# Gate and up products in swapping 64-row tiles, with a new order of work, in a transformer block of linear-memory attention and a gated feed-forward

## The chip, the cores and the metric

The kernel runs on one NeuronCore of a Trainium2 chip. The metric is the device time of one execution in microseconds. The engines are named as the profile names them: PE is TensorE (matmul), PEld its weight loads, DVE is VectorE, ACT is ScalarE, POOL is GpSimd, SP is SyncE, which here issues DMAs.

## What is computed

The input x is 2048 rows of 448 values in bfloat16. It is normalised, goes through an attention with a memory carried over four segments of 512 rows, and through a gated feed-forward of width 1792; the two results are multiplied and added to x.

```python
xn = layernorm(x)
# attention, 16 heads of 28, segments s = 0..3 of 512 rows
q, k, v = xn @ wq, xn @ wk, xn @ wv
phi = lambda t: where(t > 0, t + 1, exp(t))
for s in range(4):
    p = softmax(qs @ ks.T * 28**-0.5 + causal_mask)
    a_mem = (phi(qs) @ M) / (phi(qs) @ z + 1e-6)
    o = g * a_mem + (1 - g) * (p @ vs)
    M, z = M + phi(ks).T @ vs, z + phi(ks).sum()
s = o @ wo
g = silu((gelu(xn @ w_gate) * (xn @ w_up)) @ w_down)
return x + s * g
```

## The kernel before

Everything is done by segments of 512 rows. A segment has 4 blocks of 128 rows. The 448 input columns are the contraction of the projections and of gate/up: three chunks of 128 rows of weights and a rest of 64.

The work is written as about a thousand small operations (class `Op`, line 26), each with its engine or engines, an estimated time, the operations that it needs, the buffers that it takes and a priority. The function `arrange` (line 276) is a list scheduler that runs when the program is built: it plays the operations against estimated engine times, takes at each step the one of best priority among those that could start within `AHEAD`, assigns buffers and PSUM banks, and returns the operations in order of their planned start. They are issued to the engines' queues in that order, so each queue's order is fixed, and a wait that comes out longer on the chip than planned holds all that is behind it on that engine. Two tables steer this: `PRIO` (line 87) gives a priority to each operation by name, and `STEP` (line 258) says after which step of the attention's scores a piece of PE work may start. They were found by a search over the planner's own time.

The stages follow each other as G0, A0, A1, G1, A2, G2, A3, G3, D3 (`ORDER`, line 273).

- An A stage (`attention`, from line 960) is ten steps of scores (line 985, four heads at once in 32-row tiles), each followed by exps on ACT (line 1000), masks on POOL (line 1011), and four groups of products with v (line 1047, four 32-column tiles). The probabilities go to `pt` buffers, five of them. Between the scores PE does other work: projections of a later segment (line 714), the down products of an earlier one (line 1155), the output projection (line 1185), the memory's update (line 860) and read (line 898).
- A G stage (`gate_up`, from line 1070) makes 14 blocks of 128 hidden columns. Each block takes two PSUM banks, one for gate and one for up. `full` (line 1089) does 3 chunks for gate and 3 for up, each with all 128 rows. `halves` (line 1104) does the rest of 64 rows: gate's rest lies on partitions 0 to 63 and up's on 64 to 127 of `wh_sb`, so that the two matmuls use different row tiles of the array. Four blocks' halves are done together, so that the array's tiling changes rarely: two blocks end with them and two begin with them (`VISITS`). Then ACT does the gelu (line 1114) and DVE multiplies it by up (line 1119) into `hT`.
- The projections of a segment come in pairs of blocks: 3 full chunks for each of the two (`Unit.full`), and one visit in which the two rests of 64 rows run side by side (`visit`, lines 714 to 754). Each is evicted by DVE or ACT.
- D3 is the last segment's down product and output, block by block; the last block is cut in three.

At the start, `layer_norm` of segment 0 makes two forms of x: x less its mean (`xc`, line 663), which is known early, and the normalised x (`xn`, line 653), which waits for the variance and a power on POOL (line 646). Each of the four blocks is turned by four PE transposes (line 596) and copied to `xcT` or `xnT` (line 598). All projections of segment 0 use `xcT`, and the missing factor is put in when they are evicted (lines 752 and 754); gate/up uses `xnT`. Later segments are turned by DMA transposes on SP's queue (line 685).

The first loads are issued at line 490: the first two blocks of x and the other weights by SP, the last two blocks of x and `wv` in three pieces by ACT. Each of the four segments has its own x buffer; the loads for segments 2 and 3 (line 561) are issued after the last transpose of segment 1. The residual add reads that buffer again (line 1176) at the end of each segment's work.

The planner takes 1.65 or 2.25 us from a DMA's issue to its landing, and 1.3 us of SP's queue for a DMA transpose.

```python
def halves(ends, begins):
    def mm():
        for fc in ends + begins:
            for i in range(2):
                r = slice(i * HALF, (i + 1) * HALF)
                nc.tensor.matmul(out=bf[fc].ap(i), lhsT=wh_sb[r, fc * P:(fc + 1) * P],
                                 rhs=xT.ap()[r, NC3, :], start=fc in begins, stop=fc in ends)
```

Of the kernel before, what the change touches and what calls it, by code (L numbers as in the profile page):

```python
# [15 lines left out]
ORDER = mybir.DependencyInfo(mybir.DependencyClass.NoSync, mybir.DependencyReason.DATA)  # L16
# [9 lines left out]
class Op:  # L26


    def __init__(self, name, eng, fn, deps=(), after=(), prio=0.0, mode=None, act=None, acq=(),
                 uses=(), alone=False, kb=None, rate=240.0):  # L30
        self.alone, self.kb, self.rate = alone, kb, rate
        self.name, self.eng, self.fn, self.prio = name, eng, fn, prio
        self.mode, self.act, self.acq = mode, act, list(acq)
        self.deps = [d for d in deps if d is not None]
        self.after = [d for d in after if d is not None]
        self.start = self.done = self.on = None
        for b in list(uses) + self.acq:
            b.users.append(self)
# [15 lines left out]
class Buf:  # L54
# [221 lines left out]
def arrange(ops):  # L276
# [11 lines left out]
    while ready:  # L288
# [24 lines left out]
        if e == "PE" and o.mode and o.mode != mode:  # L313
            s, mode = s + SWITCH, o.mode
# [1423 lines left out]
```

## Time and profile before

| | |
|---|---|
| time, three runs | 229.37, 230.7, 234.46 us; median 230.7 |
| span of the profiled execution, first to last instruction | 227.6 us |
| the profiled execution's own time | not shown apart; the median is 3.1 us above the span |
| PE busy | 217.5 us, 96% of the span |
| ACT, DVE, POOL busy | 152.7, 152.7, 129.3 us |
| PE clock granted | 1.0 in nearly the whole span |

A profile row in order of time gives start, length, engine, line, operation and how many were merged. A matmul's length includes its way through the array, so lengths of neighbours overlap: what a matmul costs is the distance to the next start. Brackets give the idle time of the engine before the row and what ended it. In a row of groups the numbers after the bar are the busy time in us, the mean in ns, and the idle time before. A few matmul records can be missing, so a merged row may count one matmul too few.

### The profile page before, as it was taken

The page shows a single profiled execution, that of the slowest core. Times are in us where ns is not written, and L with a number is a line of the kernel's source. Part 1 is how long each engine was busy: PE and PEld are TensorE (multiplying, and loading weights), DVE is VectorE, ACT ScalarE, POOL GpSimd, SP SyncE. Part 2 cuts the span into 40 slices and gives each one's busy share as a digit, 9 for nine tenths or more (in the row PEclk, how much of TensorE's full clock was granted, in tenths as well). Part 3 has the DMA queues.
Part 4 walks back from the last instruction along what each step waited for, and adds up shares of the span by engine and source line. Part 5 has one row for each costly group of instructions (what it writes and reads, how often), then busy time and mean ns, then how long its engine had stood idle before and what let it go on. Part 6 is the DMA issues. An engine that isn't in the chain of part 4 may idle for free.

```text
span 227.6 us, 4462 instructions
## 1 busy us (share of the span) xinstructions
PE 217.5 (96%) x1557; PEld 95.6 (42%) x1570; DVE 152.7 (67%) x287; ACT 152.7 (67%) x212; POOL 129.3 (57%) x221
## 2 busy tenths in 40 slices
PE   7999999889999999999999999999999999999991
PEld 2544433333544434344444444344444434444561
DVE  3799998767965795674875587863746463647262
ACT  4799645999898779432788898443878875346120
POOL 8601400579588599603599989853199477604500
PEclk9999999999999999999999999999999999999999
DMA  6999569964434763217603132272500018135011
GB/s 215 222 357 259 103 152 248 237 128 83 48 72 72 183 127 74 76 38 201 186 20 68 27 71 69 59 196 59 140 1 4 12 45 225 31 84 125 4 40 50
DMA packets 44708, 25.11 MB, mean 110 GB/s; under 512 B 30808, under 2 KB 40856, under 8 KB 44680
## 3 DMA queue, kind: packets, MB, share of 16 engines
q1 hardware_dynamic: 43704, 24.05, 44.7%
q10 hardware_dynamic: 976, 0.71, 1.0%
q8 instruction: 14, 0.23, 0.4%
q14 instruction: 14, 0.11, 0.2%
HBM read 16.00 MB, written 2.98 MB: 83 GB/s over the span
## 4 chain that ended last, share of the span: by engine, by line
PE 82%; ACT 10%; DVE 2%; issue 2%; ACTq 1%; POOL 1%; DVEq 0%; POOLq 0%
PE ps L1155 16%; PE ps L1089 15%; PE pp L1089 14%; PE ps L714 11%; PE pp L985 5%; PE ps L1185 5%; PE ps L1047 4%; ACT pt L1000 3%; PE ps L1104 3%; PE pp L1104 3%; PE pp L1155 2%; ACT pt L1248 2%; PE ps L898 1%; PE ps L860 1%; PE ps L1221 1%
## 5 line engine op out<-in xcount | busy, mean ns | idle before, releaser
L1000 ACT ACTIVATE pt<-pp 128x1024 bf16<-128x1024 f32 x75 | 73.3, 1037 | 11.8 <-PE pp L985 9.9
L1011 POOL TENSOR_SCALAR_AFFINE_SELECT pt<-pt 128x256 bf16<-128x256 bf16 x128 | 54.3, 448 | 26.0 <-ACT pt L1000 23.6
L1155 PE MATMUL ps<-wd_sb,hT 128*128 128x448 bf16 x182 | 39.0, 354 | 0.4 <-DVE qs L750 0.4
L1114 ACT ACTIVATE gl<-pp 128x512 bf16<-128x512 f32 x28 | 15.8, 595 | 29.0 <-PE pp L1104 23.2
L1155 PEld LDWEIGHTS <-hT 128*128 128x128 bf16 x210 | 18.8, 98 | 20.1 <-issue 5.0
L1119 DVE TENSOR_TENSOR hT<-gl,pp 128x512 bf16<-128x512 bf16 x28 | 18.4, 682 | 11.6 <-ACT gl L1114 11.5
L1119 DVE TENSOR_TENSOR hT<-gl,ps 128x512 bf16<-128x512 bf16 x28 | 18.7, 677 | 11.0 <-ACT gl L1114 8.4
L1114 ACT ACTIVATE gl<-ps 128x512 bf16<-128x512 f32 x28 | 16.6, 597 | 13.0 <-PE ps L1089 6.1
L1089 PEld LDWEIGHTS <-wu_sb 128*128 128x128 bf16 x168 | 16.4, 98 | 20.1 <-issue 0.3
L1089 PEld LDWEIGHTS <-wg_sb 128*128 128x128 bf16 x168 | 14.9, 98 | 22.5 <-issue 7.1
L909 POOL TENSOR_TENSOR om<-om,rb 128x512 f32<-128x512 f32 x12 | 14.9, 1268 | 15.9 <-DMA rb<-rdr 15.8
L714 PEld LDWEIGHTS <-xnT 128*128 128x128 bf16 (+1 forms) x192 | 15.0, 96 | 20.6 <-issue 10.1
L1089 PE MATMUL pp<-xnT,wu_sb 128*128 128x512 bf16 x84 | 22.7, 379 | 0.3
L1089 PE MATMUL ps<-xnT,wu_sb 128*128 128x512 bf16 x83 | 22.5, 379 | 0.2
L956 POOL TENSOR_TENSOR oT<-oa,om 128x512 bf16<-128x512 f32 x12 | 16.0, 1337 | 11.5 <-DVE oa L953 11.5
L1089 PE MATMUL ps<-xnT,wg_sb 128*128 128x512 bf16 x81 | 22.1, 380 | 0.3 <-issue 0.3
L1089 PE MATMUL pp<-xnT,wg_sb 128*128 128x512 bf16 x76 | 21.2, 380 | 0.4 <-issue 0.3
L831 POOL TENSOR_SCALAR e<-e 128x896 bf16<-128x896 bf16 (+1 forms) x12 | 12.8, 1070 | 10.9 <-ACT e L826 10.9
L985 PE MATMUL pp<-qT,kT 32*128 32x512 bf16 (+3 forms) x238 | 17.0, 301 | 2.0 <-ACT pt L1000 1.8
L646 POOL TENSOR_TENSOR rs<-rs,nhalf 128x1 f32<-128x1 f32 (+1 forms) x7 | 6.1, 882 | 16.1 <-DVE rs L641 16.1
L883 DVE COPY oa<-ps 128x512 f32<-128x512 f32 x16 | 10.9, 683 | 5.2 <-PE ps L1047 5.0
L1176 POOL TENSOR_TENSOR oo<-sg,x_sb 128x448 bf16<-128x448 f32 x12 | 12.4, 1037 | 2.7 <-DVE sg L1196 2.7
(121 smaller groups left out, 325.3 us busy)
## 6 DMA issues: line engine op xcount, KB each, us to landing
rb<-rdr SPq DMA_DIRECT2D x28, 256.0 KB
out_dram<-oo SPq DMA_DIRECT2D x15, 112.0 KB
wd_sb<-in_B_w_down_dram SPq DMA_DIRECT2D x2, 784.0 KB
x_sb<-in_A_x_dram SPq DMA_DIRECT2D x3, 448.0 KB
rdr<-dc SPq DMA_DIRECT2D x28, 32.0 KB
wg_sb<-in_B_w_gate_dram SPq DMA_DIRECT2D x2, 384.0 KB
wu_sb<-in_B_w_up_dram SPq DMA_DIRECT2D x2, 384.0 KB
wg_sb<-in_B_w_gate_dram SPq DMA_DIRECT2D x1, 576.0 KB
```

Source lines behind the costliest of these rows:

```text
L714: nc.tensor.matmul(out=self.bank.ap()[:, 0:D], lhsT=self.xT.ap()[r, c, n * P:(n + 1) * P], rhs=self.w[r, c, :], **kw)
L831: o = gps(f"mi{nm}{s}{half}", n / 1024, lambda: nc.gpsimd.tensor_scalar(out=t(), in0=t(), scalar1=1.0, scalar2=0.0, op0=ALU.min, op1=ALU.max),
L909: oU[s, g, 1] = t, gps(f"sm{s}{g}", 1.22, lambda t=t, r=r: nc.gpsimd.tensor_tensor(out=t.ap(), in0=t.ap(), in1=r.ap(), op=ALU.mult), deps= ...
L956: oT[s][1].append(gps(f"cb{s}{g}", 1.22, lambda g=g, t=t, tm=tm: nc.gpsimd.tensor_tensor(out=dst.ap()[:, g, :], in0=t.ap(), in1=tm.ap(), o ...
L985: nc.tensor.matmul(out=S2[i // 2].ap(i % 2)[:, c0:c0 + n], lhsT=kT[s][0].ap()[r, g, kb * P:(kb + 1) * P], rhs=qT[s][0].ap()[r, g, kb * P:L ...
L1000: nc.scalar.activation(out=dst, in_=src, func=ACT.Exp, scale=scale)
L1011: nc.gpsimd.affine_select(out=v, in_=v, pattern=[[0, 2], [1, P]], compare_op=ALU.is_ge, fill=0.0, base=0, channel_multiplier=-1)
L1089: nc.tensor.matmul(out=bf[fc].ap(i), lhsT=w[:, c, fc * P:(fc + 1) * P], rhs=xT.ap()[:, c, :], start=begins and c == 0, stop=not begins and ...
L1104: nc.tensor.matmul(out=bf[fc].ap(i), lhsT=wh_sb[r, fc * P:(fc + 1) * P], rhs=xT.ap()[r, NC3, :], start=fc in begins, stop=fc in ends)
L1114: a = act(f"ge{s}{fc}", L, lambda: nc.scalar.activation(out=gl.ap(), in_=bf[fc].ap(0), func=ACT.Gelu_apprx_tanh), func="gelu", deps=[o], a ...
L1119: nc.vector.tensor_tensor(out=hT[s][0].ap()[:, fc, :], in0=gl.ap(), in1=bf[fc].ap(1), op=ALU.mult), deps=[a] + held,
L1155: nc.tensor.matmul(out=bank.ap()[:, 0:D], lhsT=hT[s][0].ap()[:, fc, b * P:(b + 1) * P], rhs=wd_sb[:, fc, :], start=(fc == 0), stop=(fc == ...
```

## The change

1. **Gate/up.** `full` and `halves` go. Each block of hidden columns has two parts, both in 64-row tiles. Turn 0 does four chunks (three and the rest): gate on rows 0 to 63 and up on rows 64 to 127 of each chunk. Turn 1 does three chunks with the roles swapped: up on rows 0 to 63, gate on 64 to 127. The parts are interleaved: turn 0 of the next block stands before turn 1 of this one. Since turn 1 adds to the same PSUM banks from the other row tile, a one-element ACT operation (`turn_over`, planned at 0.2 us) waits for the end of turn 0 on both tiles, and turn 1 waits for it. A table `BANKS` says which pairs of banks a block may take.
2. **Projections.** A pair of blocks is one PE operation of six full chunks and one 64-row pair; the 64-row pair comes first if the array is not in the full tiling at that place, last otherwise (`flex`, `tail_first`).
3. **Segment 0.** Only blocks 0 and 2 have a centred form (`EARLY`); blocks 1 and 3 are projected from the normalised x. After each of the two groups of centred transposes stands an idle 512-column matmul (`wm`). PSUM for this part may be any of eight banks. The small pieces of `wv` are loaded by SP, not by ACT.
4. **Buffers.** Three x buffers in place of four: segment 3's x takes segment 0's. Six `pt` buffers in place of five.
5. **Order.** DMA estimates become 1.9 or 2.5 us to landing, 1.38 us for a DMA transpose (1.9 for two kinds of segment 0), engines begin at 0.8 us. The exps of phi are all held by score steps. `PRIO` and `STEP` are searched anew and all entries differ; a small term breaks ties.

The diff, cut to its core (the tables left out):

```diff
-SEM, SWITCH, TABLE, AHEAD, LATE = 0.06, 0.1, 1.29, 0.2, 0.3
+SEM, SWITCH, TABLE, AHEAD, LATE, BEGIN = 0.06, 0.1, 1.29, 0.2, 0.3, 0.8
+EARLY = (0, 2)
...
-        if e == "PE" and o.mode and o.mode != mode:
+        if e == "PE" and o.flex:
+            o.tail_first = mode != "full"
+            s, mode = s + SWITCH * (mode not in ("full", "r64")), "full" if o.tail_first else "r64"
+        elif e == "PE" and o.mode and o.mode != mode:
...
-        xs = tiles(NSEG, [P, NB, D], BF16, "x_sb")
+        x_p = slots(NSEG - 1, [P, NB, D], BF16, "x_sb")
+        xb = [Buf(x_p, [(s % (NSEG - 1),)]) for s in range(NSEG)]
...
-        pt_p = slots(5, [P, HG, L], BF16, "pt")
+        pt_p = slots(6, [P, HG, L], BF16, "pt")
...
-            return op(name, {"SP": (0.62, 1.65 if kb < 200 else 2.25)}, fn, kb=kb, **kw)
+            return op(name, {"SP": (0.62, 1.9 if kb < 200 else 2.5)}, fn, kb=kb, **kw)
...
-            return op(name, {"SP": (1.3, 1.5)}, fn, kb=200, **kw)
+            t = 1.9 if name[:3] in ("tk0", "tq0") else 1.38
+            return op(name, {"SP": (t, t + 0.9)}, fn, kb=200, **kw)
...
-                for b in range(NB):
+                for b in EARLY:
                     centred = dve(f"xc{b}", 0.32, lambda b=b: nc.vector.tensor_scalar(
...
+                    kept_warm.append(pe(f"wm{b}", [L], lambda bank=bank: nc.tensor.matmul(
+                        out=bank.ap(), lhsT=warm[:, 0:P], rhs=warm, start=True, stop=True), deps=[warm_in], after=[o],
...
-                self.scaled = s == 0
+                self.scaled = s == 0 and n in EARLY
...
+                    for c in range(NC3 + 1 - turn):
                         for i in range(2):
+                            w = wh_sb if c == NC3 else (wg_sb, wu_sb)[i ^ turn][:, c, :]
+                            m = nc.tensor.matmul(out=bf[fc].ap(i ^ turn), lhsT=w[side[i], fc * P:(fc + 1) * P],
+                                                 rhs=xT.ap()[side[i], c, :], start=not turn and c == 0,
+                                                 stop=turn == 1 and c == NC3 - 1)
+                            if not turn:
+                                ended[fc, i] = m
+                            elif c == 0:
+                                ordered(m, turns[fc])
...
+                    def turn_over():
+                        turns[fc] = nc.scalar.activation(out=idle[0:1, :], in_=nhalf[0:1, 0:1], func=ACT.Identity)
+                        for i in range(2):
+                            ordered(turns[fc], ended[fc, i])
+                    swapped[fc] = op(f"ty{s}{fc}", {"ACT": (0.2, 0.25)}, turn_over, deps=[prev], after=[nhalf_in], prio=at(ph, fc) - 401)
...
-            for ends, begins in VISITS:
-                for fc in ends:
-                    full(fc, True)
-                h = halves(ends, begins)
-                for fc in ends:
-                    hidden(fc, h)
-                for fc in begins:
-                    a = hidden(fc, full(fc, False))
+            part(0, 0)
+            for fc in range(NFC):
+                if fc < NFC - 1:
+                    part(fc + 1, 0)
+                h = part(fc, 1)
+                a = hidden(fc, h)
```

More of the change, by code (lines that the diff above doesn't have):

```diff
@@ L276, in arrange @@
 def arrange(ops):
[L279 removed]
+    free = {e: BEGIN for o in ops for e in o.eng}
     mode, table = "full", "exp"
@@ L404, in fast_path @@
         END = ONE + [(0,), (2,)]
+        EIGHT = [(i,) for i in range(8)]
         APART = [(i, j) for i in range(4, 8) for j in range(i + 1, 8)]
@@ L567, in fast_path @@
         table_op = op("table", {"ACT": (1.5, 1.6)}, lambda: nc.scalar.activation(
-            out=igate[:, 0:1], in_=nhalf[:, 0:1], func=ACT.Exp), deps=[nhalf_in], after=wv_in, prio=-400)
+            out=igate[:, 0:1], in_=nhalf[:, 0:1], func=ACT.Exp), deps=[nhalf_in], after=wv_in[:1], prio=-400)
         def warm_up():
@@ L717, in needs @@
             def needs(self, rest):
-                return self.w_in[slice(1, None) if rest else slice(0, 1)] + [self.xd[self.n]]
+                return self.w_in[slice(1, None) if rest else slice(0, 1)] + [
+                    self.xd[EARLY.index(self.n) if self.scaled else self.n]]
             def full(self):
@@ L807, in project, with mm, tails @@
                 us = [Unit(s, nm, n, -8400.0) for nm, n in pair]
-                fs = [u.full() for u in us]
-                o = visit("wr{}{}{}".format(s, *pair[0]), us, -9500.0)
-                ahead = dict(fulls=[(f, len(f.after)) for f in fs], visit=o, sc=sc, step=k)
-                pairs_ahead.append(ahead)
-        pairs_ahead = []
+                def mm(us=us):
+                    def tails(first):
+                        for u in us:
+                            u.product(NC3, start=first, stop=not first)
+                    first = o_of[us[0]].tail_first
+                    if first:
+                        tails(True)
+                    for u in us:
+                        for c in range(NC3):
+                            u.product(c, start=not first and c == 0, stop=first and c == NC3 - 1)
+                    if not first:
+                        tails(False)
+                u, nm = us[0], pair[0][0]
+                new = not u.dst[2:] and nm != "wq"
+                ns = [D] * (2 * NC3 + 1)
+                occ = sum(n / 2400 + 0.0025 for n in ns) + SWITCH
+                o = op("pj{}{}{}".format(s, *pair[0]), {"PE": (occ, occ + 0.17)}, mm, mode="full", flex=True,
+                       deps=sum((x.needs(False) + x.needs(True) for x in us), []), prio=-8400.0,
+                       acq=[x.bank for x in us] + ([u.dst[0]] if new else []), uses=[u.xT], after=u.dst[2:3])
+                o_of[u] = o
+                if new:
+                    u.dst.append(o)
+                for x in us:
+                    x.out(o)
+                pairs_of.append((o, sc, k))
+        o_of, pairs_of = {}, []
         tabled, phis = [], []
@@ L1071, in fast_path, with ordered @@
         hT = {}
-        VISITS = (((), (0, 1)), ((2, 3), (4, 5)), ((6, 7), (8, 9)), ((10, 11), (12, 13)))
+        def ordered(later, earlier):
+            tc.add_manual_dep(later.ins, earlier.ins.name, mybir.DependencyInfo(
+                mybir.DependencyClass.Sync, mybir.DependencyReason.DATA), reason="one PSUM bank, two row tiles")
         def gate_up(s, ph, rest=()):
@@ L1079, in gate_up, with part @@
             hT[s] = [Buf(hT_p), []]
-            bf = [Buf(B_, TWO if fc in (10, 11) else APART if fc > 11 else ANY) for fc in range(NFC)]
-            prev = None
-            def full(fc, begins):
+            bf = [Buf(B_, (ANY, TWO, APART)[BANKS.get(f"gu{s}{fc}", 0)]) for fc in range(NFC)]
+            prev, ended, turns, swapped = None, {}, {}, {}
+            if rest:
+                prev = visit(f"wr2{s}", list(rest), at(ph, -1), after=[att.get("sc_end")])
+            def part(fc, turn):
@@ L1084, in full @@
                 nonlocal prev
                 def mm():
-                    for i, w in enumerate((wg_sb, wu_sb)):
-                        for c in range(NC3):
-                            nc.tensor.matmul(out=bf[fc].ap(i), lhsT=w[:, c, fc * P:(fc + 1) * P],
-                                             rhs=xT.ap()[:, c, :], start=begins and c == 0,
-                                             stop=not begins and c == NC3 - 1)
-                prev = pe(f"gu{s}{fc}", [L] * 6, mm, deps=xd + gu_in[fc], after=[prev or att.get("sc_end")],
-                          prio=at(ph, fc) + 0.5, acq=[bf[fc]] if begins else [],
-                          uses=[xT] + ([] if begins else [bf[fc]]))
@@ L1213, in last_block @@
                            prio=pr - 400, uses=[bank, a])
+            starts, adds = [], []
             for h in range(len(cut) - 1):
@@ L1226, in last_block @@
                 g = act(f"th{s}{b}{h}", half, lambda r=r, ub=ub, half=half: nc.scalar.activation(
-                    out=t.ap()[:, r], in_=ub.ap()[:, 0:half], func=ACT.Silu), func="silu", deps=[o], after=silu,
+                    out=t.ap()[:, r], in_=ub.ap()[:, 0:half], func=ACT.Silu), func="silu", deps=[o], after=silu + starts[:1],
                     prio=pr - 400, acq=[] if h else [t], uses=[ub] + ([t] if h else []))
+                starts.append(g)
                 m = dve(f"y{s}{b}{h}", half / 960 + 0.065, lambda r=r: nc.vector.scalar_tensor_tensor(
```

117 lines of the change are left out of this document (58 added, 59 removed), and 377 rows, old and new, of tables (BANKS, PRIO, STEP).

## The prediction, made before the change was run

> **What bounds the kernel now.** I read the page's first two parts and the chain, then the PE rows in order of time, then who waited for whom, then the ACT rows near the places that the change touches.
>
> ```profile
> span 227.6 us, 4462 instructions
> PE 217.5 (96%) x1557; PEld 95.6 (42%) x1570; DVE 152.7 (67%) x287; ACT 152.7 (67%) x212; POOL 129.3 (57%) x221
> PE   7999999889999999999999999999999999999991
> ACT  4799645999898779432788898443878875346120
> PEclk9999999999999999999999999999999999999999
> PE 82%; ACT 10%; DVE 2%; issue 2%; ACTq 1%; POOL 1%; DVEq 0%; POOLq 0%
> ```
>
> TensorE sets the end: 82% of the chain, busy in nearly every slice, at full clock. Only three places are not PE: the first slices, a dip in slices 8 and 9, and the tail. So a change is worth what it takes from the PE stream, or what it adds to it. The sum below is made against the profiled span of 227.6 us. The profiled execution's own time outside the span is not shown; the median of the three runs, 230.7, is 3.1 us above that span, and I apply the differences to 230.7.
>
> The PE stream of a gate/up stage, in order of time (start, length, operation):
>
> ```profile
> 99.93 0.81 PE L1089 MATMUL pp<-xnT,wg_sb 128*128 128x512 bf16 x3
> 100.58 0.81 PE L1089 MATMUL pp<-xnT,wu_sb 128*128 128x512 bf16 x3
> 101.32 0.39 PE L1104 MATMUL ps<-xnT,wh_sb 64*128 64x512 bf16 x2
> 101.55 0.59 PE L1104 MATMUL pp<-xnT,wh_sb 64*128 64x512 bf16 x4
> 101.98 0.38 PE L1104 MATMUL ps<-xnT,wh_sb 64*128 64x512 bf16 x2
> 102.29 0.82 PE L1089 MATMUL pp<-xnT,wg_sb 128*128 128x512 bf16 x3
> ```
>
> Lengths overlap, so only starts count. Three full matmuls take 100.58 - 99.93 = 0.65 us, 0.216 each. Eight 64-row ones go in pairs: the starts 101.32, 101.55 and 101.98 are one pair and then two pairs apart, 0.66 for three, 0.22 a pair. So two 64-row matmuls at once cost what one full matmul costs. The borders cost more: 101.32 - 100.58 - 0.65 = 0.09 us into the 64-row tiling, and 102.29 - 101.98 - 0.22 = 0.09 out of it. That is the thing the change can take away.
>
> **The change part by part.**
>
> *Gate/up in 64-row tiles.* A block of 128 hidden columns now costs 6 full matmuls and one 64-row pair: 7 places of 0.216, 1.51 us. After, it is 4 pairs (turn 0: gate on rows 0-63, up on rows 64-127) and 3 pairs (turn 1, swapped): 7 places again. The 56 blocks go from 448 matmuls and as many loads to 784, 336 more of each, and I cost these at nothing because they run beside their partners:
>
> ```profile
> L1089 PEld LDWEIGHTS <-wg_sb 128*128 128x128 bf16 x168 | 14.9, 98 | 22.5 <-issue 7.1
> L1104 PEld LDWEIGHTS <-wh_sb 64*128 64x128 bf16 x112 | 4.4, 94 | 9.0 <-issue 5.8
> L1104 PE MATMUL ps<-xnT,wh_sb 64*128 64x512 bf16 x56 | 9.4, 378 | 0.0
> 93.00 0.73 PE L1047 MATMUL ps<-pt,vaug 128*32 128x512 bf16 x16
> 93.66 0.82 PE L1089 MATMUL ps<-xnT,wg_sb 128*128 128x512 bf16 x3
> ```
>
> The 112 narrow loads are busy 4.4 us and not 112 x 94 ns = 10.5, so they overlap. The bounds: a pair at 0.22 and not 0.216 would be 392 x 0.004 = 1.6 us. The four-at-once matmuls of line 1047 bound it higher: 0.66 us for 1280 columns, less 0.09 for a border, is 0.57 against 1280/512 x 0.216 = 0.54, some 0.009 for each of four places; 392 x 0.009 = 3.5 us. The lower end is 0. I take 0, since the pair of line 1104 is the very operation.
>
> The Trainium skill, page TensorEngine Tiling (Array Packing), section Performance Considerations, gives each matmul an overhead of about 60 cycles. Read as an addition to each, 336 more at 60/2.4 = 25 ns would be 8.4 us by estimate, and the time 235.1; the four matmuls of two pairs, 0.43 us apart from the next, do not show it, so here the measurement speaks against that reading.
>
> The borders that go: of the 16 groups of line 1104, 11 come straight after line 1089 and all 16 return to it. Those 27 vanish: 27 x 0.095 = -2.6 us. The first entry and the last exit of each stage stay (from scores, or from line 1047, either form pays a border). I counted them in the order of PE rows, of which the rows at 101.32 and 102.29 are one entry and one exit.
>
> *The turn-over.* Turn 1 writes the same two PSUM banks from the other row tile, so a tiny ACT operation waits for both ends of turn 0, and turn 1 waits for it. This is the one new wait on the path.
>
> ```profile
> 151.70 0.61 PE L1104 MATMUL pp<-xnT,wh_sb 64*128 64x512 bf16 x4
> 152.13 1.08 ACT L1114 ACTIVATE gl<-pp 128x512 bf16<-128x512 f32 x2 [2.97 <-PE pp L1104]
> 161.08 0.60 ACT L1114 ACTIVATE gl<-ps 128x512 bf16<-128x512 f32 x1 [0.70 <-PE ps L1089]
> 161.69 1.28 ACT L1000 ACT_TABLE_LOAD   x1
> 42.49 1.02 ACT L1000 ACTIVATE pt<-pp 128x1024 bf16<-128x1024 f32 x1 [0.53 <-PE ps L985]
> 43.56 0.39 PE L985 MATMUL pp<-qT,kT 32*128 32x256 bf16 x6 [1.01 <-ACT pt L1000]
> L567 ACT ACTIVATE igate<-nhalf 128x1 f32<-128x1 f32 x1 | 0.2, 203 | 0.0
> 148.00:152.00 4.00, 4.00 (x22) 1.68 (x22) 3.01 (x6) 1.11 (x2) 1.35 (x2) 1.00 0.81 226
> 16.00:20.00 4.00, 3.84 (x21) 1.68 (x19) 3.83 (x8) 3.97 (x6) 0.93 (x1) 1.00 1.20 363
> 44.00:48.00 4.00, 3.65 (x33) 1.53 (x35) 3.93 (x12) 4.00 (x7) 3.15 (x8) 1.00 0.67 105
> ```
>
> A gelu starts 0.43 us after its matmul's start, or 0.21 after that matmul's place ends (152.13 against 151.70). A one-element ACTIVATE is 0.20. With 0.05 back to PE (an exp ends at 42.49 + 1.02 = 43.51, scores start at 43.56), turn 1 is allowed 0.46 us after turn 0 ended. In between PE does turn 1 of the block before (3 x 0.216 = 0.65) and turn 0 of the next (0.86): 1.51 us. So 1.05 us are to spare; one gelu (0.60) ahead in ACT's queue is hidden, one exp of 1.0 nearly, a table load of 1.28 is not. In a quiet stage ACT is 1.11 of 4 us busy (in a window's row the busy times are PE, weight loads, DVE, ACT, POOL); 2 to 3 turns a window add 0.5. The cover is thin only where ACT is full: 3.97 of 4 in the first segment. What queues behind a late turn-over is the gelu of the block before, and behind turn 1 all of PE. Bounds: 0 (never late), or every one of 56 late by some 0.2 us (half a gelu pitch), 11.2 us. I take 0.6, near 0, because the spare time exceeds a gelu in all but the first microseconds of each stage. If the operation's function forced a table load each time, it would be ruinous (56 x 1.28 = 72 us and more); no row shows it between gelus, and at line 752 the same function runs among exps without a load. The Trainium skill, page ScalarE: Activation LUTs, section Table sets: the hidden batching unit, has identity in every set, so no load by it; no run here shows that. I give it no chance of its own.
>
> *Projection pairs in one operation, 64-row part first or last.* 18 pairs of segments 1 to 3 now go full, 64-row, next. Entered after scores and followed by full work, tail-first saves one border. At most 8 of the present groups are followed by full work: 0 to -0.8; I take half, -0.4.
>
> *Start.* Blocks 1 and 3 of the first segment lose their centred copy, its four transposes and eviction; two idle matmuls come in, and two small weight loads move from ACT's queue to SP's.
>
> ```profile
> 1.33 1.70 ACTq L490 DMA_DIRECT2D wv_sb<-in_A_wv_dram  x3
> 3.06 1.28 ACT L567 ACT_TABLE_LOAD   x1 [3.06 <-issue]
> 4.46 0.56 ACT L615 ACTIVATE hT<-x_sb 128x448 bf16<-128x448 bf16 x1
> 5.58 1.05 ACT L598 COPY xnT<-ps 128x512 bf16<-128x512 bf16 x2
> 6.20 0.74 PE L714 MATMUL ps<-wv_sb,xnT 128*128 128x448 bf16 x3 [0.20 <-ACT xnT L598]
> 6.78 0.39 PE L596 MATMUL ps<-oT,hT 128*128 128x128 bf16 x4
> 7.00 0.39 PE L596 MATMUL pp<-oT,hT 128*128 128x128 bf16 x4
> ```
>
> On PE eight transposes go (two groups, each 7.00 - 6.78 = 0.22, -0.44) and two 512-column matmuls come (+0.43): nothing. ACT issues one weight DMA and not three, so its table load starts about 1.1 us earlier (two of three in 1.70). The first projection at 6.20 waited for ACT's copy at 5.58, which stood behind the sums that began at 4.46. Bounds 0 and -1.1; the transposes before it leave about half: -0.5. On SP two issues (about 0.57 each) now stand ahead of all later loads; those land 1.1 us later, hidden by the projections unless the gate weights are late.
>
> *Order, sixth probability buffer, DMA times.* PE's own waits are few:
>
> ```profile
> PE pp L985 <- ACT pt L1000: 1.8, 3, 1.0
> PE ps L1155 <- DVE qs L750: 0.4, 1, 0.4
> 41.31 5.53 SPq L763 DMA_TRANSPOSE kT<-kn  x4
> ```
>
> 2.2 us, in the first attention stage, where ACT is 4.00 of 4. The new planner gives a transpose 1.38 us, which is the row (5.53/4). Against it, the second exp of phi(k) of segment 0 is now held until after the first scores and so moves into the ACT-bound stage, 1.0 us each for one or two. Bounds: -2.2 to +2.0. I take -1.1: the new delays are nearer to the rows, and a sixth buffer lets exps run on when POOL's masks are late. The buffer and the wider PSUM choices cost nothing.
>
> *Three x buffers.* The load of segment 3's x now waits for the last residual add of segment 0, on SP's in-order queue; behind it are the den/rdr/rb transfers of segment 1.
>
> ```profile
> 36.15 0.39 SPq L561 DMA_DIRECT2D x_sb<-in_A_x_dram  x1
> 113.30 1.04 POOL L1176 TENSOR_TENSOR oo<-sg,x_sb 128x448 bf16<-128x448 f32 x1 [2.41 <-DVE sg L1196]
> 116.56 1.59 PE L714 MATMUL ps<-wk_sb,xnT 128*128 128x448 bf16 x8
> ```
>
> Now that load is issued at 36.15, a residual add of segment 0 runs as late as 113.30, and segment 3's first projection is at 116.56. Load, statistics and four transposes (4 x 1.38 = 5.5) can't fit in 3 us, so the order must bring the finish of segment 0 forward, which it can: the first attention stages hold the work. Segment 3's two wk pairs are also held until the fifth and sixth of the stage's ten score steps have begun, so PE has other work before them. Bounds 0 to +10; I take 0.
>
> Sum: -2.6 - 0.4 - 0.5 - 1.1 + 0.6 + 0 = -4.0, so 230.7 - 4.0 = 226.7.
>
> **The rivals.**
> - *The order does better*: all waits go (-2.2), the start gives all (-1.1), tail-first gives 0.8 and turn-overs cost nothing: -2.6 - 0.8 - 1.1 - 2.2 = -6.7, 224.0. For it: the waits are known and the new delays match. Against: the ACT-bound stage gets an exp.
> - *The pair costs more than a place* (0.009 each, +3.5): 230.2; the change then does nothing that shows. For it line 1047, against it line 1104.
> - *Turn-overs come late*: ACT's in-order queue holds PE up 0.2 us in each of 56 turns: +11.2 in place of +0.6, so 230.7 - 4.6 + 11.2 = 237.3. It decides from 0.08 us a turn on (4.6/56: no gain) and at 0.16 (9.2/56) it is 2% slower. For it 3.97 of 4 us at 16-20, against it 1.11 of 4 at 148-152.
> - *Segment 3's x comes late*: PE waits some 6 us for its projections, 232.7.
>
> **How the numbers follow.** About 2% is what a measurement of this kernel tells from no change: 226.1 and 235.3. Forecast 0.47 (its own range 224.5 to 229), better order 0.27, costlier pair 0.10, late turn-overs 0.10, late x 0.06. Faster: the better order and 0.09 of the forecast's lower part, 0.36. Slower: late turn-overs and a little of late x, 0.13. Within 2%: the rest, 0.51. The range 221.8 to 233.0 leaves out late turn-overs and the ends of the others.
>
> **What would show it.** Right: gate/up matmuls all 64*128, 784 of them, pairs 0.216 apart, no gap of 0.09 inside a stage; 56 ACT operations of 0.2 us; PE rows with waits for ACT's idle tile under 1 us in all; the first projection near 5.7. Wrong: PE waits for that tile of several us, above all in the first segment; pairs further apart than 0.22; a PE wait before segment 3's projections; a wait of scores for exps above 2.2 us.

## The result, and the profile after

The changed kernel takes 840.84 us (median of 6 runs, 838.82 to 842.5), the kernel before 230.12 us on the same chip (6 runs, 229.37 to 234.46). The ratio is 3.652, 95% interval 3.643 to 3.660. Predicted were 226.7 us and a range of 221.8 to 233.0. The ratios here and below leave out some slower executions, most of them 1 to 2% longer and one of the kernel before at 1213.53 us, which nothing here explains.

610 us more is no wait of PE that somebody mis-sized. The first lines of the page say so: not the same work takes longer, there is three times as much work.

```profile
span 839.3 us, 13363 instructions
...
PE 675.6 (80%) x4812; PEld 333.8 (40%) x4812; DVE 506.9 (60%) x1153; ACT 466.7 (56%) x879; POOL 207.7 (25%) x331
...
PE   8999999999538677892877689396878948687896
...
PEclk9999999999859555896955579685557978655798
```

13363 instructions stand against 4462, 4812 matmuls against 1557. Slices 1 to 10 (21 us each) look like the page of before; from slice 11 on, PE has holes and a lower clock. Cut at 226 us, by the view of stretches (length, then busy time and count of PE, weight loads, DVE, ACT, POOL, granted clock, DMA share, GB/s):

```profile
0.00:224.00 224.00, 218.73 (x1900) 98.93 (x1900) 153.95 (x286) 161.92 (x265) 129.43 (x221) 1.00 0.47 111
224.00:226.00 2.00, 0.00 (x0) 0.00 (x0) 0.50 (x3) 0.00 (x0) 0.00 (x0) 0.93 0.33 90
226.00:839.00 613.00, 456.82 (x2912) 234.90 (x2912) 352.44 (x866) 304.81 (x614) 78.31 (x110) 0.71 0.06 17
```

The first 224 us hold all 1900 matmuls of the planned kernel. The 2912 behind belong to other lines, as the rows in order of time at the border show:

```profile
224.56 0.34 SPq L1291 DMA_DIRECT2D out_dram<-oo  x1
224.56 0.38 ACTq L1291 DMA_DIRECT2D out_dram<-oo  x1
226.38 0.34 SPq L1489 DMA_DIRECT2D beta_bf<-in_A_beta_dram  x1
226.40 0.14 DVE L1484 MEMSET bdmask<- 96x96 f32 x1 [1.87 <-DMA out_dram<-oo]
```

At 224.56 the planned path stores its last rows. At 226.38 the kernel loads its inputs anew: these lines belong to a second function, `general_path` (from line 1431), which computes the whole output again without the planned path's shortcuts. It stands behind a branch at the end of both kernels, and the section on the kernel before did not speak of it:

```python
ok = fast_path(...)                 # L1755
with tc.If(ok == 1) as common:      # L1757
    pass
with common.Else():
    general_path(...)
```

`ok` is a flag that the planned path computes on the side. A guard squares wq and wk, sums them by head and compares the product with a limit, so that the softmax may leave out its maximum. The sums go into `red`, and `red` is a part of the tile `um`, which the memory updates of segments 1 and 2 write later:

```python
red = um[:, 0, :].rearrange("p (i n) -> p i n", i=2)     # L454
# guard: red <- sums of squares (L1306); matmul over um[:, 0, :] (L1313), then the flag
# update, s >= 1:  um <- new products * bdmask (L926);  macc += um (L929)
```

The view of the tile `um`, first of the kernel before, then of the changed one (shortest, median and longest in ns; start of the first and the last in us):

```profile
L1251 DVE TENSOR_REDUCE um<-pt x8: 579/601/611, 12.2 to 24.0; 128x16 f32<-128x448 bf16 x6, 64x16 f32<-64x448 bf16 x2
...
L1258 PE MATMUL ps<-um,ones x2: 270/270/271, 32.0 to 32.1; 128*1 128x128 f32 x2
L872 DVE TENSOR_TENSOR um<-ps,bdmask x2: 681/686/691, 78.8 to 139.0; 128x512 f32<-128x512 f32 x2
```

```profile
L1306 DVE TENSOR_REDUCE um<-pt x8: 602/608/611, 12.0 to 32.3; 128x16 f32<-128x448 bf16 x6, 64x16 f32<-64x448 bf16 x2
L926 DVE TENSOR_TENSOR um<-ps,bdmask x2: 680/685/690, 84.7 to 114.4; 128x512 f32<-128x512 f32 x2
...
L1313 PE MATMUL ps<-um,ones x2: 270/270/271, 174.7 to 174.8; 128*1 128x128 f32 x2
```

Read the starts from top to bottom. Before: sums 12.2 to 24.0, the guard's matmul at 32.0, updates at 78.8 and 139.0. After: sums 12.0 to 32.3, updates at 84.7 and 114.4, and only then, at 174.7, the guard's matmul. It reads the numbers of an update. One entry of the new priority table, `"nrm": 1060`, put it there; the planner tracks buffers of its pools, but `um` is a constant tile that it knows nothing of, so no edge held the order.

### The profile page after: what moved, and what is told of

Its sections match the earlier page's. It is cut to its first block, busy times and chain, and to the rows that moved or that the text cites. A ratio compares the mean times of both kernels' runs of the same rounds, so it can differ in the third digit from the quotient of the medians.

```text
span 839.3 us, 13363 instructions
## 1 busy us (share of the span) xinstructions
PE 675.6 (80%) x4812; PEld 333.8 (40%) x4812; DVE 506.9 (60%) x1153; ACT 466.7 (56%) x879; POOL 207.7 (25%) x331
## 5 line engine op out<-in xcount | busy, mean ns | idle before, releaser
L1633 PE MATMUL tp<-ident,p_sb 128*128 128x128 bf16 x640 | 103.0, 292 | 24.0 <-ACT p_sb L1624 21.0
L1618 DVE TENSOR_REDUCE mx<-big 128x2 f32<-128x256 f32 (+3 forms) x128 | 104.3, 815 | 1.5
L1639 ACT COPY pt_sb<-tp 128x128 bf16<-128x128 bf16 (+3 forms) x128 | 54.5, 426 | 61.7 <-PE tp L1633 57.3
L1633 PEld LDWEIGHTS <-p_sb 128*128 128x128 bf16 x640 | 55.1, 122 | 46.5 <-ACT p_sb L1624 42.9
L1610 PE MATMUL big<-kT,qT 32*128 32x128 bf16 (+3 forms) x256 | 62.7, 422 | 13.4 <-ACT p_sb L1624 12.7
L1614 DVE TENSOR_TENSOR big<-big,cmask 128x256 f32<-128x256 f32 x128 | 55.0, 430 | 25.1 <-PE big L1610 14.0
L1641 PE MATMUL acc<-vaug,pt_sb 128*128 128x29 bf16 x640 | 56.4, 192 | 12.6 <-ACT pt_sb L1639 5.7
L1720 PE MATMUL big<-xnT,wg_sb 112*128 112x512 bf16 x224 | 62.9, 396 | 0.0
L1720 PE MATMUL big<-xnT,wu_sb 112*128 112x512 bf16 x224 | 61.5, 385 | 0.0
L1147 PE MATMUL ps<-xnT,wu_sb 64*128 64x512 bf16 x180 | 47.3, 376 | 0.0
```

Of the source, the lines that this page charges most:

```text
L1147: m = nc.tensor.matmul(out=bf[fc].ap(i ^ turn), lhsT=w[side[i], fc * P:(fc + 1) * P], rhs=xT.ap()[side[i], c, :], start=not turn and c == ...
L1610: nc.tensor.matmul(out=s_ps[:, i, 0:w], lhsT=qT[hh * HP:(hh + 1) * HP, g, j * P:(j + 1) * P], rhs=kT[hh * HP:(hh + 1) * HP, g, 0:w], start ...
L1614: nc.vector.tensor_tensor(out=s_ps[:, :, j * P:w], in0=s_ps[:, :, j * P:w], in1=cmask[:].unsqueeze(1).to_broadcast([P, 2, P]), op=ALU.add)
L1618: nc.vector.reduce_max(out=mx[:], in_=s_ps[:, :, 0:w], axis=AX.X)
L1633: nc.tensor.transpose(pt_ps[:, kb, :], p_sb[:, i, kb * P:(kb + 1) * P], ident[:])
L1639: nc.scalar.copy(out=pt_sb[:, 0:j + 1, :], in_=pt_ps[:, 0:j + 1, :])
```

## The experiments

The theory (A): the flag is 0 because the guard reads `um` after the updates wrote over the sums; the 610 us are the second path. The rivals: the planned path itself is slower (B), another part of the change makes the flag 0 (C), the late place alone does (D). Four kernels ran together with the kernel before (229.77 us).

**no_fallback**: the changed kernel, second path left out.

```diff
-    with common.Else():
-        general_path(tc, ...)
```

> The changed kernel with the second path left out of the branch's other side, so that only the planned path runs; its order is that of the changed kernel, instruction for instruction. Theory A (the time over 230 us is the second path, which runs because the guard's flag reads 0): 229 to 231 us, since the planned path's last vector operation ends at 224.3 us in the changed kernel's trace and at 224.0 in that of before. Rival B (the second path is there, but the planned path is itself slower than its trace shows, since its end is hidden behind the second path's start): 232 us or more. The prediction's own figure for the planned path is 226.7.

Measured: 228.70 us, ratio 0.9948 (0.9930 to 0.9966). All of the 610 us is the second path, and rival B falls. The planned path by itself is 0.5% faster than the kernel before, which still has its branch, and 2.0 us slower than the 226.7 predicted.

**early_sums**: one number.

```diff
-    "nrm": 1060,
+    "nrm": 100,
```

> The changed kernel with one number of the priority table changed, so that the guard's matmul is issued soon after the last of its sums (planned at 30.2 us) and not after the two memory updates (174.7 in the trace). Theory A (the updates write over the sums, which lie in the same tile, before the guard's matmul reads them): the flag is 1, nothing runs after 228 us, 229 to 231.5 us. Rival C (another part of the change makes the flag 0: the tiles of 64 rows, the centred blocks, the buffers): 835 to 845 us as before.

Measured: 230.72 us, ratio 1.0050 (1.0031 to 1.0070). The tile's rows are in the old order again:

```profile
L1306 DVE TENSOR_REDUCE um<-pt x8: 599/606/614, 11.5 to 31.8; 128x16 f32<-128x448 bf16 x6, 64x16 f32<-64x448 bf16 x2
...
L1313 PE MATMUL ps<-um,ones x2: 270/270/271, 32.7 to 32.8; 128*1 128x128 f32 x2
L926 DVE TENSOR_TENSOR um<-ps,bdmask x2: 680/686/691, 85.3 to 115.0; 128x512 f32<-128x512 f32 x2
```

The second path does not run. Theory A holds, rival C falls. That it is 2 us slower than no_fallback comes up again below.

**before_late**: the kernel before, guard behind the first update.

```diff
     o = dve(f"um{s}", ..., uses=[u])
+    if s == 1:
+        ok_op.deps[0].deps.append(o)
```

> The kernel before with one edge added to its plan: the guard's matmul waits for the first memory update (planned at 109.7 us in place of 31.0). Theory A: the sums are gone by then, the flag is 0 and the second path of some 612 us is added: 835 to 850 us, with nothing of the change in it. Rival C (another part of the change makes the flag 0): 230 to 232 us, the planned path being 0.9 us longer by the plan.

Measured: 842.97 us (two runs), ratio 3.666 (3.655 to 3.677). Without any part of the change, the one edge makes the same 613 us:

```profile
L872 DVE TENSOR_TENSOR um<-ps,bdmask x2: 683/688/692, 78.7 to 139.4; 128x512 f32<-128x512 f32 x2
...
L1260 PE MATMUL ps<-um,ones x2: 271/272/272, 111.6 to 111.7; 128*1 128x128 f32 x2
```

**late_unshared**: the guard stays behind the first update, but the updates leave `um` alone, and VectorE does the add that GpSimd did.

```diff
-    out=um[:], in0=uv(), in1=bd, op=ALU.mult)
+    out=uv(), in0=uv(), in1=bd, op=ALU.mult)
-    nc.gpsimd.tensor_tensor(out=macc[:], in0=macc[:], in1=um[:], op=ALU.add)
+    nc.vector.tensor_tensor(out=macc[:], in0=macc[:], in1=uv(), op=ALU.add)
```

> The changed kernel with the guard's matmul still behind the first memory update (planned at 85.7 us against 81.4), but the updates no longer write the tile that holds the sums: the masked product stays in PSUM and VectorE adds it, where GpSimd did. Theory A (writing over the sums is the cause): the flag is 1, 229 to 235 us (the plan is 3.7 us longer). Rival D (the late place by itself is the cause, in whatever tile the sums lie): 835 to 850 us.

Measured: 234.43 us (two runs), ratio 1.0195 (1.0157 to 1.0233). The guard's matmul ran at 89.2, behind the update at 84.6 (now `ps<-ps`), and the second path did not:

```profile
L926 DVE TENSOR_TENSOR ps<-ps,bdmask x2: 689/694/699, 84.6 to 115.6; 128x512 f32<-128x512 f32 x2
...
L1313 PE MATMUL ps<-um,ones x2: 270/270/271, 89.2 to 89.3; 128*1 128x128 f32 x2
```

So lateness alone does not make the second path run; D falls. Late and shared is 841 and 843, early and shared 230.7, late and unshared 234.4: it takes both. The cause of the result is settled.

The second question is where the 4 us went that the planned path was to gain. A branch with a second path also costs something when it is not taken, so the kernel before needs the same cut.

**before_no_fallback** (the Else left out of the kernel before).

> The kernel before without its second path, the like of no_fallback, so that the two planned paths are compared without the branch's jump. If the jump costs the kernel before what its rows say (last store issued at 224.64 and the span over 2.96 us later, against 2.62 in no_fallback): 229.3 to 229.6 us against 229.8. If the branch costs it more, so that no_fallback's gain of 0.5% is the branch alone: 228.6 to 228.9.

Measured: 229.45 us, ratio 0.9963 (0.9930 to 0.9995). Like against like, 0.9948 against 0.9963: the change is worth some 0.3 us, which these intervals don't tell from nothing.

The PE starts of both traces, from the first projection to the last matmul, give the balance. I took each distance between starts and split it into the place of the matmul, the border where the tiling changes, and the rest, a stall; the places of missing matmul records are put back. The rows are rounded:

| from before to no_fallback | before | no_fallback | difference, us |
|---|---|---|---|
| borders between tilings | 155, 15.6 us | 123, 12.4 us | -3.2 |
| stalls in all | 2.9 us | 5.2 us | +2.3 |
| of these before the first scores | 0.5 us | 2.7 us | +2.2 |
| first projection | 6.20 | 6.70 | +0.5 |
| places of matmuls: eight transposes fewer behind it | | | -0.4 |
| start of the last matmul | 222.69 | 221.86 | -0.8 |

The gain at the borders is there in full. The start takes most of it back: the first scores begin at 38.66 before and at 40.22 here, 1.6 us later. The traces of before_no_fallback and of the changed kernel, 38.98 and 40.58, give the same 1.6. The last matmul is less certain: before_no_fallback, the same planned order as the kernel before, starts it at 223.33 and not at 222.69. The waits of PE, with the total, number and longest in us, first before, then no_fallback:

```profile
PE pp L985 <- ACT pt L1000: 1.8, 3, 1.0
PE ps L572 <- DVE oT L525: 1.3, 1, 1.3
PE ps L1155 <- DVE qs L750: 0.4, 1, 0.4
```

```profile
PE ps L598 <- DVE oT L551: 1.2, 1, 1.2
PE ps L745 <- DMA wv_sb<-in_A_wv_dram: 0.9, 1, 0.9
PE pp L1147 <- DVE hT L1173: 0.4, 1, 0.4
PE pp L622 <- DVE xn L680: 0.3, 1, 0.3
PE ps L745 <- DVE hT L1173: 0.3, 1, 0.3
PE pp L745 <- DVE kn L786: 0.3, 1, 0.3
PE ps L1039 <- ACT pt L1054: 0.2, 1, 0.2
```

The scores' wait for exps (1.8) is nearly gone (0.2). In its place stand waits for wv, for the normalised x of block 1 and for its evictions. The one for wv comes and goes with the execution: 1.7 us in early_sums, none in the changed kernel's own trace, where PE waits 0.6 us for `xn` in place of 0.3.

Half of the 2.7 us, some 1.3, lies elsewhere: in segment 0's gate/up, from 17.8 to 33.4 us, where PE stands still six times before a part. Before the longest of them, 0.6 us, the profile names VectorE's product of an earlier block:

```profile
24.09 0.37 PE L1147 MATMUL pp<-xnT,wg_sb 64*128 64x512 bf16 x1 [0.44 <-DVE hT L1173]
```

The trace of fill_waits below has the same six. The kernel before has none there but for its guard's matmul (0.3 us). That the new order of parts holds its PSUM banks longer is a guess that no run tests.

The wait for `xn` has an odd row:

```profile
9.39 1.17 DVE L680 TENSOR_SCALAR xn<-x_sb,mv,rs 128x448 bf16<-128x448 bf16 x1
...
10.69 0.39 DVE L680 TENSOR_SCALAR xn<-x_sb,mv,rs 128x448 bf16<-128x448 bf16 x1
```

```profile
10.61 0.58 PE L622 MATMUL pp<-oT,xn 128*128 128x128 bf16 x4 [0.34 <-DVE xn L680]
```

The same operation takes 1.17 us and, 1.3 us later, 0.39. Beside the long one GpSimd's fill of wo_sb ran. In the kernel before the same fill ran at the very start; the new order moved it. First the row of no_fallback, then that of before:

```profile
8.59 1.59 POOL L551 MEMSET wo_sb<- 128x1792 bf16 x1
```

```profile
1.24 1.59 POOL L525 MEMSET wo_sb<- 128x1792 bf16 x1
```

The long operation ended at 10.56, 0.38 us after the fill, about its own length.

**fill_waits**: that fill waits for the normalisation of the third block, which comes behind the second's; the order unchanged, the second path left out.

```diff
-wo_z = fill("POOL", "wo0", 1.55, -70, wo_sb[:], 0.0)
+wo_z = op("wo0", {"POOL": (1.55, 1.61)}, lambda: tc.add_manual_dep(
+    nc.gpsimd.memset(wo_sb[:], 0.0).ins, made[0, 2].ins.name, ...), prio=-70)
```

> The changed kernel without its second path, order unchanged, but GpSimd's zero fill of wo_sb (1.59 us from 8.59 us on) waits for the normalisation of x's second and third block on VectorE, as the plan has it in time but no semaphore says. Theory G (GpSimd's fill holds VectorE's write of xn, 1.17 us where the same operation takes 0.39 beside no fill; PE waits 0.3 to 0.5 us for it at 10.6): that xn takes 0.39 and 0.2 to 0.6 us are saved, 228.1 to 228.5 against 228.7. Rival H (the wait moves to the next late piece, the 64-row products at 13.8): 228.6 to 228.9.

Measured: 228.01 us, ratio 0.9905 (0.9869 to 0.9941). The first scores begin at 39.20 in place of 40.22.

```profile
9.07 0.39 DVE L683 TENSOR_SCALAR xn<-x_sb,mv,rs 128x448 bf16<-128x448 bf16 x1
...
9.59 0.39 DVE L683 TENSOR_SCALAR xn<-x_sb,mv,rs 128x448 bf16<-128x448 bf16 x1
```

```profile
10.04 1.59 POOL L582 MEMSET wo_sb<- 128x1792 bf16 x1 [1.08 <-DVE xn L683]
10.55 1.11 DVE L707 COPY xn<-xn 128x64 bf16<-128x64 bf16 x1
```

The fill starts at 10.04, behind them. The normalisation takes 0.39 again and PE's wait for it is gone, as theory G says; the gain, 0.7 us between the medians, is a little over its 0.2 to 0.6. The fill now stretches the next copy (1.11 us, where the one at 9.49 took 0.18), which PE does not wait for. Of the 1.0 us at the first scores 0.3 is an earlier first projection (6.37), since this execution had no wait for wv. But four traces of the new order that had none either, with the fill in its old place, begin the first scores at 40.6 to 41.0 (the changed kernel, hint_later, hint_act_only, fall_true), so the fill's share is some 1 us all the same. At the last matmul 0.9 is left (220.96 against 221.86), and PE had another wait here, 0.8 us for a load of w_down. The intervals of the two ratios overlap, so this time alone would not show it; the same edit made on early_sums (repaired, below) does.

**all_centred**: the segment-0 part undone, the second path left out. The guard's matmul is also put before the updates here, by `"nrm": 100` and an edge, in lines that are not shown.

```diff
-EARLY = (0, 2)
+EARLY = (0, 1, 2, 3)
+o.prio = RANKS[k]      # priorities searched anew for this set of operations
```

> The changed kernel without its second path, with the segment-0 part undone: all four blocks of the first segment are projected from centred x again (EARLY is 0 to 3), and the priorities searched anew for it; its plan ends at 223.16 us against 221.43 for no_fallback, first scores at 38.1 against 37.6. In no_fallback the chip began the first scores at 40.22, 2.6 us behind its plan; in the kernel before at 38.66, 1.3 behind. Theory P (the blocks projected from normalised x are what is late at the start, since they wait for GpSimd's square root and VectorE's normalisation): first scores 1.3 us behind plan again, at 39.2 to 39.7, and 228.7 + 1.7 - 1.3 = 229.1 us, 228.6 to 229.6. Rival Q (the start is late for another reason, such as the loads): first scores at 40.5 to 41, 230.0 to 230.8 us.

Measured: 228.55 us, ratio 0.9940 (0.9906 to 0.9974); first scores at 39.14, 1.05 us behind its plan. These are theory P's numbers, and with a plan 1.7 us longer the chip is as fast as no_fallback. But the new search moved the fill too: it runs at 1.17 here, as at 1.24 in the kernel before. So this kernel has no fill beside a normalisation either, and fill_waits, which keeps the normalised blocks, reaches the first scores at 39.20. The fill explains both runs; that the normalised blocks cost something of their own is not shown. What they promise at the start, 0.5 us by the plan (37.6 against 38.1), the chip does not give: 39.20 against 39.14.

**turn_x3**: the disputed wait, made longer.

```diff
-turns[fc] = nc.scalar.activation(out=idle[0:1, :], ...)
+for k in range(3):
+    turns[fc] = nc.scalar.activation(out=idle[0:1, :], ...)
```

> The changed kernel without its second path, with each of the 56 turn-over operations on ScalarE issued three times in a row, so that each turn is over some 0.2 to 0.4 us later; order and everything else as in no_fallback (228.7 us). Theory E (the turn-over is hidden: 1.05 us to spare in the prediction, so only the turns of the crowded first segment can show): 228.5 to 230.5 us. Rival F (it is on PE's path in every turn): 56 x 0.2 to 0.4, 240 to 251 us.

Measured: 235.05 us, ratio 1.0202 (1.0152 to 1.0253), 6.3 us more than no_fallback: between the two theories, and in the range of neither. The three take 0.65 us in a row, so each turn is over 0.45 later, and 56 x 0.45 would be 25 us. PE's waits for it are 4.0 us, in nine places of the 56; the other 2 us are not taken apart:

```profile
PE ps L1147 <- ACT nhalf L1160: 2.6, 7, 0.8
PE pp L1147 <- ACT nhalf L1160: 1.4, 2, 0.7
```

First some places of turn_x3, then one of no_fallback:

```profile
96.56 1.28 ACT L1169 ACT_TABLE_LOAD   x1
...
98.34 0.65 ACT L1160 ACTIVATE nhalf<-nhalf 1x1 f32<-1x1 f32 x3
...
99.05 0.39 PE L1147 MATMUL ps<-xnT,wu_sb 64*128 64x512 bf16 x1 [0.77 <-ACT nhalf L1160]
...
115.92 0.39 PE L1147 MATMUL ps<-xnT,wu_sb 64*128 64x512 bf16 x1 [0.18 <-ACT nhalf L1160]
```

```profile
101.39 0.20 ACT L1159 ACTIVATE nhalf<-nhalf 1x1 f32<-1x1 f32 x1 [0.33 <-PE ps L1147]
...
102.64 0.38 PE L1147 MATMUL ps<-xnT,wu_sb 64*128 64x512 bf16 x1
```

In no_fallback the turn is over at 101.59 and needed at 102.64: the 1.05 us to spare of the prediction. Most turns have this; the first few of a stage have 0.2 to 1.0, the last 0.2, and the tightest of all, in segment 0, 0.06. In turn_x3 it is gone where a table load stands ahead (0.77) and in the last block of a stage, which has no next turn 0 between (the distance there is longer by 0.34). These two places come back in every stage. At its real size the turn-over is hidden: PE's waits of no_fallback do not name it. Only weight loads wait for it, 1.3 us in six places, ahead of their matmuls.

**early_sums is 2 us slower than no_fallback**: why? Part of it is at the end. Rows of the trace that the profile's views leave out (start in us, engine, instruction):

```
before       223.98 Vector COMPARE_BRANCH   224.59 Vector EVENT_SEMAPHORE
before       224.66 Scalar COMPARE_BRANCH   225.16 Scalar EVENT_SEMAPHORE
early_sums   224.27 Vector COMPARE_BRANCH   224.87 Vector EVENT_SEMAPHORE
early_sums   224.96 Scalar COMPARE_BRANCH   228.03 Scalar EVENT_SEMAPHORE
```

ScalarE needs 3.07 us from its branch to its next instruction, where the kernel before needs 0.50; all engines wait for it. SyncE, which gathers the others, stands 0.98 us at this wait, so about 1 us of the 2 is the jump. The last matmul of early_sums also starts 0.6 us later than no_fallback's (222.43 against 221.86), which is no more than two traces of one order differ (222.69 and 223.33). Both kernels give ScalarE and VectorE a hint of the branch some 64 us ahead. Three kernels tried to move it.

**hint_later** (`near` is "dn330a" in place of "sc30").

> early_sums (230.7 us), with the hint that fetches the instructions behind the branch given at about 207 us of the plan and not at 161. Theory J (the jump over the second path costs: ScalarE took 3.07 us from its branch at 224.96 to its next instruction, 0.50 us in the kernel before, and the hint given 64 us ahead no longer holds after 110 recorded instructions on ScalarE, 86 before): ScalarE's jump takes 0.5 us again and 1 to 1.5 us are saved, 229.2 to 229.8. Rival K (the hint is not what differs): 230.4 to 231.

Measured: 230.96 us, ratio 1.0017 (0.9988 to 1.0047). ScalarE's hint is at 209.34 and its jump still takes 2.97 us. Rival K.

**hint_act_only** (`engines=[Activation]` in place of `[Activation, DVE]`).

> early_sums (230.7 us) with the hint given to ScalarE alone and not to VectorE too. Theory L (the hint that comes second to the chip is lost: VectorE's came first in the changed kernel, 160.58 against 161.45, and ScalarE's in the kernel before): ScalarE's jump takes 0.5 us in place of 3, VectorE's becomes long; VectorE branches 0.7 us earlier, so the end gains at most 1 us, 229.7 to 230.5. Rival M (ScalarE's hint fails for a reason of its own code): its jump stays at 3 us and VectorE's becomes as long, 230.7 to 231.5.

Measured: 230.70 us, ratio 1.0026 (1.0001 to 1.0051). ScalarE 2.68, VectorE 2.90 us. The hint works for VectorE (0.60 with it) and not here for ScalarE. Rival M.

**fall_true** (`preferred_fallthrough_block=True`).

> early_sums (230.7 us) with the other block laid behind the branch (the flag that chooses the fallthrough block turned round). Theory N (the wait of 3 us is for instructions that lie behind the second path, so the layout decides it): no engine takes over 1 us from its branch to its next instruction, 228.9 to 229.7 us. Rival O (the second path lies between in either layout): 230.4 to 231 us.

Measured: 230.69 us, ratio 1.0035 (1.0017 to 1.0053). The first branch is short now (ScalarE 0.11), but the block ends in another over the second path: ScalarE 2.79, VectorE 3.09. Rival O. Why the hint to ScalarE holds in the kernel before and in none with the new order stays open; its place in ScalarE's own code is only a guess.

**repaired**: early_sums and fill_waits together, with the second path kept.

> The changed kernel with its second path kept, the guard's matmul early (early_sums) and GpSimd's fill behind the normalisation (fill_waits). Theory: the two add, 230.7 - 0.4 to 1.0 = 229.7 to 230.3 us, so no better than the kernel before, since ScalarE's jump of 3 us stays. Rival (the fill's wait was worth less than the trace of fill_waits shows): 230.4 to 231.

Measured: 229.61 us, ratio 0.9980 (0.9961 to 0.9998), 0.1 below the expected range. Against early_sums (1.0050, 1.0031 to 1.0070) the intervals lie apart, so the time shows the fill too; the first scores are at 39.23. Against the kernel before it is level, 0.2% ahead at the very edge of the interval. ScalarE's jump (2.75 us) is still in it.

## Why the prediction was wrong

- *Order, sixth probability buffer, DMA times* is the step that failed. It took a new order for a matter of waits ("Bounds: -2.2 to +2.0. I take -1.1"). But an order written by priorities also decides which of two uses of one tile comes first where the planner has no edge. It moved the guard's matmul from 32.0 to 174.7 us, past two writes of its source (before_late, late_unshared). The prediction costs the order as waits alone and follows no moved step to what else writes its tile.
- The branch behind the planned path appears in no term and no rival. Its price, some 613 us, was not in the trace of before, since it did not run; that it existed was in the code.
- *Borders*, -2.6 and -0.4: 32 fewer, -3.2 us. Right, and for the reason given.
- *The pair costs a place*: right; the distances between 64-row pairs in no_fallback's gate/up have a median of 0.216 us. That rival is gone. The overhead of some 60 cycles a matmul in the Trainium skill, page TensorEngine Tiling (Array Packing), section Performance Considerations, is not added in these pairs.
- *Turn-over*, +0.6 within 0 to 11.2: PE waits for it in no row of no_fallback's list, and the table loads are 11 in both traces, as the Trainium skill, page ScalarE: Activation LUTs, section Table sets, has it for identity. The spare time of 1.05 us is what most turns have. The cover is thin behind a table load, as the prediction says, and in the last block of a stage, which it does not name; turn_x3 shows both, and at its real size the turn-over does not reach them.
- *Start*, -0.5: mis-sized, with the wrong sign. The sign to look for was a first projection near 5.7; it came at 6.70 in no_fallback, at 5.9 to 7.3 in the other traces of the new order, and at 6.20 before. The first scores come 1.6 us later (40.22 against 38.66). I costed what was taken from PE and ACT, not that blocks 1 and 3 now wait for a square root on GpSimd and a normalisation on VectorE before PE can turn them, nor that the new order puts GpSimd's fill beside that normalisation. Some 1 us is this fill (fill_waits, repaired). Another 1.3 us are the stalls in segment 0's gate/up, which stand in no term ("The buffer and the wider PSUM choices cost nothing"); their cause stays open.
- *The waits for exps*, -1.1 within -2.2 to +2.0: 1.8 became 0.2, but stalls between the first scores of segments 0 and 2 went from 1.9 only to 1.6 us, as waits for hT came in. No run separates the sixth buffer from the new delays.
- *Three x buffers*, 0: right; no wait for segment 3's x.

So the mechanism named for the gain was there, -3.2 us, the start gave most of it back, and a thing outside the sum added 610. That the planned path by itself (228.70) lies in the forecast's own range of 224.5 to 229 is in part luck: it has no second path to jump over, and with the path, and the guard in time, it is 230.72 (early_sums).

## What to carry to other kernels

A priority table or a searched order is safe only for the hazards that the planner knows: before costing a new order, list the tiles that have two uses without an edge and see which use comes first. Look for a branch or a second path at the end of a kernel, and ask of each moved step whether the flag can depend on it. Where a plan relies on two operations not overlapping, as the fill and the normalisation here, a semaphore has to say so: planned times alone did not keep them apart.

## What the runs showed of the hardware

- GpSimd's fill of 128x1792 bf16 stretched a VectorE TENSOR_SCALAR between SBUF tiles from 0.39 to 1.17 us, to 0.38 us past the fill's end; with the fill moved behind, 0.39. The moved fill stretched a 128x64 copy between SBUF tiles from 0.18 to 1.11.
- A change of PE's tiling cost 0.10 us (155 changes, 15.6 us, before; 123, 12.4 us, in no_fallback).
- A branch over a long block not run costs an engine 0.5 to 3.5 us until its next instruction (TensorE 3.47 in fall_true; VectorE 0.60 with a hint and 2.90 without; ScalarE 0.50 in the kernel before, 2.7 to 3.1 with a hint in every kernel of the new order that keeps the second path and does not run it).
- In the second path, with PE busy 457 of 613 us, the granted clock was 0.71 on the mean; in the planned path, busy 219 of 224 us, it was 1.00.
